# A block-sparse attention and gated MLP kernel: a planner's order replaced by a written list

## The chip, the cores and the metric

The kernel runs on one core of a Trainium2 chip. The core has a matrix engine (TensorE, here PE; its weight loads are shown as PEld), a vector engine (VectorE, DVE), an activation engine (ScalarE, ACT), a general engine (GpSimd, POOL) and a queue engine that only issues DMAs (SyncE, SP). Each engine takes its own instructions strictly in the order in which the program gives them; between engines, semaphores make one wait for another. Matrix results go to eight banks of PSUM, of 2 KB in each of 128 partitions. The metric is the device time of one execution in microseconds; lower is better.

## The reference

Four batches, eight heads, 768 positions of 64 numbers. Attention is block-sparse with blocks of 32 positions: a query block sees the block itself and its two neighbours, the first and the last block, and three blocks given at run time by `sampled_blocks`. The first and the last query block see everything. The attention output is then the input of a two-layer MLP over 3072 tokens.

```python
scores = scale * np.matmul(q, k.transpose(0, 1, 3, 2))
mask = np.abs(blk_i - blk_j) <= window          # window = 1
mask = mask | (blk_i == 0) | (blk_j == 0) | (blk_i == n_blocks - 1) | (blk_j == n_blocks - 1)
for qb in range(n_blocks):
    for kb in sampled_blocks[qb]:
        mask[qb * block:(qb + 1) * block, kb * block:(kb + 1) * block] = True
attn = softmax(np.where(mask, scores, -1e9))
x = np.matmul(attn, v)                          # then heads side by side: (3072, 512)
h = x @ w_in                                    # (3072, 2048)
g = h * (1.0 / (1.0 + np.exp(-beta * h)))
out = g @ w_out                                 # (3072, 512)
```

## The kernel before, in words

The work is cut into 1731 *tasks*. A task has a name, an engine (or two from which one is chosen), a guessed duration, the tasks that it depends on, the PSUM banks that it opens or closes, and a function that records its instructions, mostly one to a few dozen. The kinds, in the order in which data passes through them:

- `ldK`, `ldV`, `ldQ`: loads of half a batch's K, V or Q. For batch 0 they are issued on SP (768 KB each), for batches 1 to 3 on POOL. `castK`, `castQ`, `vperm`, `permV` on DVE turn them to 16 bits; `trK`, `trQ` transpose on PE (L632), `evK`, `evQ` evict (ACT or DVE). `vtab` writes V to a table in HBM, from which `vg` gathers the value blocks (SP; `vv` loads the block numbers into registers).
- `selb`, `selw`, `sel16`, `pick`, `pickv`: for the first four pairs the sampled value blocks are instead picked by a matmul with a selection matrix (L825). `mask`, `maskb`, `maskc` make the additive mask for doubled blocks.
- Attention works on 44 *pairs* of query blocks (11 per batch), all heads at once. For pair n: `kg` (POOL, L710) copies the sampled key blocks, `kn` (POOL or DVE) the fixed ones; `sc` is the score matmuls (mask L849, then L862; from pair 33 on some are done two pairs at a time); `mx` the row maxima (DVE, L884), `ex` the exponentials (ACT, L892); `hl` or `rc` the reciprocals (DVE); `nrm` the scaling (POOL or DVE, L915, from pair 11 on); `tp` eight transposes on PE (L929) and `ptv` their copy out (DVE or ACT); for pairs from 31 on one transposing DMA `tpd` on SP does both; `av` the product with the values (L971, from pair 16 on the wide form of L963; before pair 11 with the reciprocals' matmuls of L953); `rs`, `xv` put the result into the transposed activations `xT` (DVE or ACT). Buffers limit how far pairs can run ahead: three for keys and for probabilities, four or eight for values.
- The first and last block of a batch go through `gs`, `gm`, `ge`, `gr`, `gn`, `gt`, `gptv`, `gav`, `gx`, four units to a batch.
- The MLP takes the tokens in groups of 8, 8, 8, 16, 16, 16, 16 and 8 blocks of 32. For group G and each of 16 slices f, `hG.f` is four matmuls (L1155), `tanh` is on ACT (L1161), `stt` on DVE (L1166); then `yG.s.part`, four parts of four matmuls of 512 columns per 128 tokens (L1182), `oe` scales (ACT, L334) and `od` stores. `win` and `wout` are the weight loads, issued on POOL.

What sets the order: class `Plan` holds an event simulation. At each moment it gives each free engine the ready task with the lowest rank; the rank is a priority plus an offset from a table of tuned numbers. It chooses between two engines by which ends sooner by its guessed durations, and gives a task that opens banks the ones that are free longest. At most five banks go to the MLP while attention is left. The resulting order of tasks is then recorded, so that each engine has its instructions in that order. The plan's times have no effect beyond that order, the choice of engines and the banks.

Of the kernel before, what the change touches and what calls it, by code (L numbers as in the profile page):

```python
# [20 lines left out]
BIAS = {("nrm", "DVE"): 2.0, ("gn", "DVE"): 1.5}  # L21


class Task:
    def __init__(self, name, eng, dur, emit, deps=(), prio=0.0, lat=0.0,
                 opens=(), closes=(), moe=False, dma=0.0, slack=0.0, hw=0, bulk=None):
        self.on = {eng: dur} if isinstance(eng, str) else dict(eng)
        self.name, self.eng, self.dur, self.emit = name, None, None, emit
        self.deps = [d for d in deps if d is not None]
# [4 lines left out]
        self.tiling = Plan.TILING.get(self.kind, 0)  # L34
        self.end = None


class Plan:


    HOP = 0.18
# [3 lines left out]
    MARGIN, DMARGIN = 1.0, 1.0  # L45


    TILING = {"sc": 1, "gs": 1, "av": 2, "gav": 2, "trK": 2, "trQ": 2}
    CHANGE, KEEP = 0.1, 0.0
    YOUNG = {"PE": 0, "DVE": 0, "ACT": 0.0, "POOL": 0.5, "SP": 0.0}  # L50
    YIELD = 20

    OFFSET = {'gt': 5, 'gav': 10, 'trK': 7.6, 'oe': 2.2, 'vg': -0.6, 'vv': -14.0, 'pick': -1.2, 'av0': 0.8, 'ptv0': -3.8, 'xv0': 3.7, 'vg0': 0.9, 'sc1': -2.5, 'kg1': 12.5, 'kn1': -11.1, 'mx1': -15, 'vg1': -5, 'av2': -5, 'kg2': 2.8, 'kn2': 4.2, 'hl2': 5.2, 'rs2': -5, 'kg3': -11.2, 'ex3': 0.3, 'rs3': -0.6, 'kg4': -15, 'rs4': 7.8, 'kn5': 18.1, 'ptv5': 6.3, 'rs5': 39.6, 'av6': -0.3, 'kg6': 2.5, 'kn6': -60, 'ptv6': -2.4, 'mx6': 4.5, 'sc7': 15.7, 'tp7': 21.7, 'av7': 1.3, 'rs7': 1.6, 'sc8': 0.4, 'hl8': -3.7, 'xv8': -17.7, 'av9': -14.9, 'kg9': -6.0, 'kn9': 15, 'mx9': -15, 'ex9': -0.6, 'hl9': 19.8, 'rs9': 15, 'sc10': 21.3, 'tp10': 0.8, 'av10': 15, 'kg10': 2.9, 'kn10': -15, 'mx10': 30, 'vg10': 30, 'sc11': -60, 'av11': 15, 'ex11': 5, 'xv11': -1.7, 'av12': 0.5, 'kn12': -2.5, 'ptv12': 1.2, 'rs12': -0.3, 'xv12': 26.5, 'tp13': -0.2, 'kn13': 4.0, 'rs13': -3.7, 'xv13': -41.1, 'av14': 15, 'kg14': -15, 'kn14': -30, 'rs14': 24.8, 'xv14': 6.6, 'ptv15': 30, 'xv15': -24.7, 'mx0.0': 0.7, 'mx0.1': -9.9, 'mx1.1': -3.1, 'ex1.1': 5.7, 'ex2.0': -2.1, 'ex4.1': -15, 'mx7.1': 56.3, 'gn1': -22.5, 'vperm0.0': -0.6, 'trQ1': 11.7, 'trQ2': 11.1, 'trK3': 2.2, 'trQ3': -0.4, 'castQ': 2.6, 'tabK2': -34.6, 'tabK3': 8.6, 'ttQ2': 19.9, 'ldV3': 0.9, 'pick1': 9.2, 'pickv': 30, 'ldV0.1': 0.1, 'evK0': -6.3, 'evQ0': -1.2, 'tanh0': 5.1, 'stt1': -14.2, 'h3': 0.5, 'y3': -1.4, 'oe3': -8.0, 'y4': 1.4, 'tanh4': 9.0, 'oe4': 1.7, 'h5': 15.9, 'y5': -1.2, 'stt5': 3.2, 'h6': -60, 'y6': 11.9, 'tanh7': 60, 'stt7': -19.4}

    def __init__(self, n_banks, moe_banks):
        self.tasks = []
        self.n_banks, self.moe_banks = n_banks, moe_banks
        self.bank = {}
# [6 lines left out]
    def run(self):  # L65
        tasks = self.tasks
        attention_left = sum(1 for t in tasks if t.opens and not t.moe)
        succ = {}
        need = {}
        for t in tasks:  # L70
            need[t] = len(t.deps)
            for d in t.deps:
                succ.setdefault(d, []).append(t)
        readers = {}
        for t in tasks:
            for b in t.closes:
                readers[b] = readers.get(b, 0) + 1
        ready_at = {t: 0.0 for t in tasks}
        engines = sorted({e for t in tasks for e in t.on})
        free = {e: 0.0 for e in engines}  # L80
        waiting = {e: [] for e in engines}
        ring_at = hw_at = 1.0
        lanes = [0.0] * 8
        issued = 0

        tiling = 0
        off = {t: t.prio + self.OFFSET.get(t.name, self.OFFSET.get(t.name.split(".")[0], self.OFFSET.get(t.kind, 0.0)))
               for t in tasks}

        def rank(t, e):  # L90

            young = now - ready_at[t] < self.YOUNG[e] - 1e-9
            return off[t] + (self.KEEP if e == "PE" and t.tiling != tiling else 0.0) + (self.YIELD if young else 0.0)

        bank_free = [(0.0, i) for i in range(self.n_banks)]
        held_moe = 0
        moe_owner = set()
        events = []
        seq = 0

        def release(t):
            for e in t.on:
                waiting[e].append(t)

        for t in tasks:
            if need[t] == 0:
                release(t)
        now = 0.0
        order = []
        done = 0  # L110
        while done < len(tasks):
            progress = False
            for e in engines:
                if free[e] > now + 1e-9:
                    continue
                best = None
                for t in waiting[e]:
                    if ready_at[t] > now + 1e-9:
                        continue
                    if len(t.on) > 1:  # L120
                        cost = {o: max(free[o], now) + d + BIAS.get((t.kind, o), 0.0)
                                for o, d in t.on.items()}
                        if cost[e] > min(cost.values()) + 1e-9:
                            continue
                    if t.bulk is not None and ring_at > now + t.bulk + 1e-9:
                        continue
                    if t.opens:
                        n_ok = sum(1 for f, _ in bank_free if f <= now + 1e-9)
                        if n_ok < len(t.opens):
                            continue  # L130
                        if t.moe and attention_left and held_moe + len(t.opens) > self.moe_banks:
                            continue
                    if best is None or rank(t, e) < rank(best, e):
                        best = t
                if best is None:
                    continue
                t = best
                for other in t.on:
                    waiting[other].remove(t)
                t.eng, t.dur = e, t.on[e] * (1.0 if e == "PE" else self.MARGIN)  # L140
                if e == "PE" and t.tiling != tiling:
                    t.dur += self.CHANGE
                    tiling = t.tiling
                if t.opens:
                    bank_free.sort()
                    for name in t.opens:
                        _, i = bank_free.pop(0)
                        self.bank[name] = i
                        if t.moe:
                            held_moe += 1  # L150
                            moe_owner.add(name)
                    if not t.moe:
                        attention_left -= 1
                free[e] = now + t.dur
                end = now + t.dur + t.lat
                if t.hw:
                    at = now
                    for _ in range(t.hw):
                        at = max(at, lanes[issued % 8]) + t.dur / t.hw
                        begin = max(hw_at, at + 0.4)  # L160
                        both = max(0.0, ring_at - begin) / self.RING
                        work = self.DMARGIN * t.dma / t.hw
                        took = work / self.DIRECT if work <= both * self.DIRECT else work + both * (1 - self.DIRECT)
                        ring_at += (1 - self.RING) * min(took, both)
                        hw_at = begin + took
                        end = lanes[issued % 8] = hw_at + 0.9 + (self.LATER if ring_at > hw_at else 0.0)
                        issued += 1
                    free[e] = at
                elif t.dma:
                    begin = max(ring_at, end + 0.6)  # L170
                    both = max(0.0, hw_at - begin)
                    work = self.DMARGIN * t.dma
                    took = work / self.RING if work <= both * self.RING else work + both * (1 - self.RING)
                    ring_at = begin + took
                    end = ring_at + 1.1
# [1082 lines left out]
```

## Time and profile before

| | |
|---|---|
| runs shown | 300.73, 301.71, 305.26 us; median 301.71 |
| the profiled execution's span | 302.9 us (from the first to the last instruction) |
| busy PE | 279.5 us, 92%, 4109 matmuls |
| busy DVE, ACT, POOL | 237.5, 218.6, 170.0 us |
| mean granted clock of PE | 0.981 |
| DMA | 47.55 MB, mean 157 GB/s |

The profile is of one execution, of which the span is the time from the first to the last instruction; the durations used below are from it. Busy PE includes time in which a matmul's end is only modelled, so a busy PE need not be at its peak. A stretch's row gives each engine's busy time in it and the number of instructions, then the clock granted to PE as a share of full speed. A row of a group of instructions gives line, engine, operation, what is written from what, shapes and count, then the busy time and the mean of one in ns, then the idle time just before them and what ended it. A row in order of time gives the start and duration in us.

### The profile page before, as it was taken

The numbers are of one execution on the slowest core, as the hardware profiler recorded it, in microseconds if no ns is written. First come the engines' busy times: TensorE is split into PE (matmuls) and PEld (weight loads), VectorE is DVE, ScalarE is ACT, GpSimd is POOL, SyncE is SP. The second block draws the span as 40 slices with busy tenths as digits, with TensorE's granted clock in tenths as the row PEclk, the third lists the DMA queues.
The fourth block names the chain that finished last, engine by engine and source line by source line (L and its number), as shares of the span: only waits on it lengthen the run. The fifth ranks groups of instructions, "written<-read, shape, count | busy, mean of one in ns | idle before, by whom it ended". The sixth has DMA issues, their size and how long they took to land.

```text
span 302.9 us, 11451 instructions
## 1 busy us (share of the span) xinstructions
PE 279.5 (92%) x4109; PEld 173.8 (57%) x4109; DVE 237.5 (78%) x556; ACT 218.6 (72%) x641; POOL 170.0 (56%) x513
## 2 busy tenths in 40 slices
PE   2599879999998799999999999999999999999993
PEld 1465668758846576665556555545554544555671
DVE  5848987999899998999999739999888834762150
ACT  3357657888789598799889749896787768763360
POOL 5057995034579957899777538677976654000000
PEclk9999957999999999999999999999999999999999
DMA  7999999979978852299933643248465446541102
GB/s 248 365 294 171 205 232 231 228 142 265 213 126 167 181 192 72 84 173 162 237 99 106 202 154 106 67 110 167 120 158 119 126 106 181 137 121 53 53 36 69
DMA packets 57170, 47.55 MB, mean 157 GB/s; under 512 B 19733, under 2 KB 53142, under 8 KB 57114
## 3 DMA queue, kind: packets, MB, share of 16 engines
q1 hardware_dynamic: 44736, 35.48, 41.3%
q0 software_dynamic: 12320, 11.27, 24.7%
q8 instruction: 32, 0.52, 0.7%
q14 instruction: 24, 0.20, 0.2%
q10 hardware_dynamic: 58, 0.07, 0.1%
HBM read 45.23 MB, written 9.44 MB: 180 GB/s over the span
## 4 chain that ended last, share of the span: by engine, by line
PE 49%; DVE 23%; issue 7%; ACT 6%; POOL 6%; DMA 5%; POOLq 2%; SPq 0%; DVEq 0%; ACTq 0%
PE bank L1155 17%; PE bank L1182 14%; DVE ST L884 5%; PE bank L825 4%; DVE g L1166 4%; PE bank L929 3%; POOL KG L710 3%; DMA g<-in_k_dram 3%; DVE SG L1040 3%; POOL PP L915 2%; PE bank L963 2%; PE bank L971 2%; ACT PP L892 2%; PE bank L632 2%; ACT t L1161 2%
## 5 line engine op out<-in xcount | busy, mean ns | idle before, releaser
L1155 PE MATMUL bank<-xT,w_in_sb 128*128 128x256 f16 (+1 forms) x512 | 93.8, 330 | 1.5 <-DVE g L1166 1.5
L892 ACT ACTIVATE PP<-bank,ST 128x256 f16<-128x256 f32 x176 | 81.9, 482 | 15.1 <-DVE ST L884 10.1
L1182 PE MATMUL bank<-w_out_sb,g 128*128 128x512 f16 x384 | 92.0, 379 | 0.0
L1161 ACT ACTIVATE t<-bank,beta_sb 128x512 f16<-128x512 f32 (+1 forms) x128 | 71.0, 595 | 15.7 <-PE bank L1155 10.4
L915 POOL TENSOR_SCALAR PP<-PP,ST 128x256 f16<-128x256 f16 x132 | 63.4, 499 | 30.8 <-DVE ST L909 29.2
L1166 DVE SCALAR_TENSOR_TENSOR g<-t,bank 128x512 f16<-128x512 f16 (+1 forms) x128 | 67.0, 547 | 16.3 <-ACT t L1161 15.8
L1155 PEld LDWEIGHTS <-w_in_sb 128*128 128x128 f16 x512 | 54.4, 115 | 28.1 <-issue 4.1
L710 POOL COPY KG<-KT 128x64 f32 x264 | 52.4, 249 | 25.6 <-PE bank L862 10.5
L884 DVE TENSOR_REDUCE ST<-bank 128x2 f32<-128x512 f32 x88 | 57.6, 680 | 4.2 <-PE bank L862 3.8
L1182 PEld LDWEIGHTS <-g 128*128 128x128 f16 x384 | 35.0, 98 | 37.4 <-issue 3.5
L892 ACT ACTIVATION_READ_ACCUMULATOR PP<-bank,ST 128x1 f32 x176 | 37.4, 212 | 0.0
L1061 POOL TENSOR_SCALAR PG<-PG,SG 128x768 f16<-128x768 f16 x13 | 13.1, 1010 | 24.4 <-ACT PG L1049 15.2
L334 ACT ACTIVATE osb<-bank 128x512 f32<-128x512 f32 (+1 forms) x24 | 14.2, 590 | 16.1 <-PE bank L1182 16.0
L330 DVE COPY PT<-bank 128x1024 f16<-128x1024 f16 x30 | 20.4, 683 | 3.8 <-PE bank L929 3.6
L330 DVE CAST xT<-bank 64x256 f16<-64x256 f32 (+1 forms) x35 | 14.6, 418 | 9.9 <-PE bank L963 6.8
L929 PE MATMUL bank<-identity,PP 128*128 128x128 f16 x248 | 20.4, 225 | 1.2 <-ACT KT L328 0.6
L963 PEld LDWEIGHTS <-VG 128*128 128x128 f16 x448 | 16.1, 98 | 9.2 <-issue 4.3
L1049 ACT ACTIVATE PG<-bank,SG 128x384 f16<-128x384 f32 x32 | 18.3, 589 | 4.2 <-DVE SG L1042 3.6
L929 PEld LDWEIGHTS <-PP 128*128 128x128 f16 x248 | 16.2, 101 | 6.0 <-issue 1.1
L963 PE MATMUL bank<-PT,VG 128*128 128x64 f16 x448 | 17.5, 193 | 2.2 <-DMA PT<-PP 1.5
L330 POOL COPY KG<-KT 128x384 f32<-128x384 f32 (+3 forms) x43 | 16.6, 411 | 1.3 <-PE bank L862 1.3
L328 ACT CAST xT<-bank 64x256 f16<-64x256 f32 (+1 forms) x30 | 11.3, 375 | 8.2 <-PE bank L1089 3.9
(119 smaller groups left out, 317.9 us busy)
## 6 DMA issues: line engine op xcount, KB each, us to landing
VG<-VT SPq DMA_DIRECT2D x220, 32.0 KB, 2.6
VG<-VT SPq DMA_DIRECT2D x32, 192.0 KB, 2.7
out_dram<-osb SPq DMA_DIRECT2D x20, 256.0 KB, 2.1
RV<-in_v_dram POOLq DMA_DIRECT2D x6, 384.0 KB, 6.6
RK<-in_k_dram POOLq DMA_DIRECT2D x6, 384.0 KB, 6.2
VT<-Vn SPq DMA_DIRECT2D x3, 768.0 KB, 3.4
RQ<-in_q_dram POOLq DMA_DIRECT2D x6, 384.0 KB, 6.3
w_in_sb<-in_moe_w_in_dram POOLq DMA_DIRECT2D x8, 256.0 KB, 8.8
```

What stands on the lines that cost most here:

```text
L330: (nc.vector if eng == "DVE" else nc.gpsimd).tensor_copy(out=out, in_=in_)
L710: nc.gpsimd.tensor_copy(out=kg32[:, g, :, (SR + r) * W:(SR + r + 1) * W], in_=kt32[:, :, bass.ds(vals[3 * g + r], W)])
L884: mx[n, u] = add(f"mx{n}.{u}", "DVE", 0.6, lambda n=n, u=u, sb_=sb_: nc.vector.tensor_reduce(out=sb_[:, 0, 2 * u:2 * u + 2], in_=bank(("S" ...
L892: nc.scalar.activation(out=pb[:, u, g, :], in_=bank(("S", n, u))[:, g * 256:(g + 1) * 256], func=AF.Exp, bias=sb_[:, 0, 2 * u + g:2 * u + ...
L915: (nc.vector if eng == "DVE" else nc.gpsimd).tensor_scalar(out=pb[:, u, g, :], in0=pb[:, u, g, :], scalar1=sb_[:, 2, 2 * u + g:2 * u + g + ...
L929: nc.tensor.transpose(out=o[:, s * P:(s + 1) * P], in_=pb[:, u, g, c * P:(c + 1) * P], identity=identity)
L963: nc.tensor.matmul(o[:, (g * NHP + hp) * 2 * BLK:(g * NHP + hp + 1) * 2 * BLK], lhsT=vgb[:, g, c, hp * P:(hp + 1) * P], rhs=pt[:, g, c, :, ...
L1049: nc.scalar.activation(out=pg[:, :].rearrange("x (j p) -> x j p", j=J)[:, :, hf * hw_:(hf + 1) * hw_], in_=bank(("GS", m, hf))[:, 0:S // 2 ...
L1155: nc.tensor.matmul(o[:, 0:TW], lhsT=w_in_v[:, c, f // 4, f % 4, :], rhs=xT[:, c, c0:c0 + TW], start=(c == 0), stop=(c == NHP - 1))
L1161: lambda G=G, f=f, TW=TW, tt=tt: nc.scalar.activation(out=tt[:, 0:TW], in_=bank(("H", G, f))[:, 0:TW], func=AF.Tanh, bias=0.0, scale=beta_ ...
L1166: lambda G=G, f=f, TW=TW, tt=tt, gg=gg: nc.vector.scalar_tensor_tensor(out=gg[:, f, 0:TW], in0=tt[:, 0:TW], scalar=1.0, in1=bank(("H", G, ...
L1182: nc.tensor.matmul(o[:, :], lhsT=gg[:, f, s * P:(s + 1) * P], rhs=w_out_sb[:, f, :], start=(f == 0), stop=(f == N_FFC - 1))
```

## The change

The event simulation goes. A string, ORDER, lists all 1731 tasks by name, each with the engine (A, D, G for ACT, DVE, POOL) where there is a choice, and with the PSUM banks that it opens. `Plan.run` reads the list, sets engine and banks, and returns the tasks in that order. The guessed durations in the task definitions change too, but nothing reads them any more; a new task kind for loading key block numbers ahead is defined and switched off (`NKL = 0`). So the instructions are the same apart from the form that an engine needs, and what differs is the order on each engine, the engine of 93 tasks, and the banks.

```diff
+ORDER = """
+selc sbl ldK0.1 ldK0.0 ldV0.1 ldV0.0 ldQ0.0 idx srow ident iota selb0:0 castK0.2 castK0.3 selb1:1 selw0 mask.0
+trK0.3:2 selw1 evK0.3:A sel16.2 castK0.0 sel16.0 trK0.0:2 castK0.1 evK0.0:A sel16.4 trK0.1:1 vperm0.1 trK0.2:0
...
+tpd33 gm15 y3.2.3 xv31.1:D kg37 ge15 vg34.0 nrm34:D h4.12:7 vg35.3 vg35.4 oe3.3 av32:5 gm14 h4.10:2 vres34:G xv32.0:A
...
+stt7.15 stt7.13 y7.0.2 stt7.14 y7.0.3 y7.1.1 oe7.0 y7.1.2 od7.0 y7.1.3 rows:6 oe7.1 of7.1 rowlist od7.1ACT od7.1SP
+"""
...
-    OFFSET = {'gt': 5, 'gav': 10, 'trK': 7.6, ...
...
     def run(self):
-        tasks = self.tasks
-        attention_left = sum(1 for t in tasks if t.opens and not t.moe)
...
+        by = {t.name: t for t in self.tasks}
+        full = dict(A="ACT", D="DVE", P="PE", G="POOL", S="SP")
         order = []
...
+        for word in ORDER.split():
+            name, _, place = word.partition(":")
+            t = by[name]
+            t.eng = full[place[0]] if place and place[0] in full else next(iter(t.on))
+            t.dur = t.on[t.eng]
+            for b, i in zip(t.opens, place.lstrip("ADPGS")):
+                self.bank[b] = int(i)
+            order.append(t)
         return order
...
-    plan = Plan(8, 5)
+    plan = Plan()
```

How the list stands against the old order, in the parts that the prediction speaks of:

- Start: the loads of batch 0 are in the order K, K, V, V, Q, then (behind the V table's two stores) Q; before it was V, V, K, K, Q, then Q behind the stores. The dummy activation `table` moves from the start to the middle; the ACT table load itself stays ahead of ACT's first copy.
- PE up to `sc0`: four `trK`, `pick1.0`, `trQ0.0`, `pick1.1`, `maskb`, `pick0.0`, three `trQ`, `pick2.1`, then `sc0`. `rows` moves from the start of PE's queue to its very end, `betaT` behind `av2`.
- PE's order between attention and MLP: up to `av12` the old order had 36 `h` and 16 `y` tasks, the new one 18 `h` and no `y`. In the old order `h0.0` came after `av4`, in the new one after `sc10`. The last MLP groups are interleaved differently, with `y` of groups 5 and 6 among `h` of 6 and 7.
- POOL: the weight loads (`win`, `wout`) are spread between the `kg` of pairs 3 to 17, with loads of batch 1 among them; before, all sixteen stood ahead of `kg11`.
- Engines of tasks: `ptv` 12 from DVE to ACT and one back; `xv` 15 from DVE to ACT, 11 back; `evK`, `evQ` 7 to ACT, 4 to DVE; `pickv` 2 to ACT, one back; `rs` 2 to ACT, 3 back; `nrm` 7 from POOL to DVE; `kn` 12 from DVE to POOL, 7 back; `vres` 3 from DVE to POOL; `gn` three each way.
- Eight banks as before, dealt from the list.

More of the change, by code (lines that the diff above doesn't have):

```diff
@@ L43 @@
     DIRECT, RING, LATER = 0.25, 0.7, 2.5
-    MARGIN, DMARGIN = 1.0, 1.0
     TILING = {"sc": 1, "gs": 1, "av": 2, "gav": 2, "trK": 2, "trQ": 2}
[L49 to L53, printed above, removed]
@@ L80, in run @@
[L80 to L93, printed above, removed]
```

362 lines of the change are left out of this document (173 added, 189 removed).

## The prediction

> **What bounds the kernel now.** I read the granted clock first, then busy time by stretch, then the chain of waits, then the instructions of the first 42 us in order of time. The stretches, busy time of each engine (instructions in brackets), granted clock, DMA share and GB/s:
>
> ```profile
> core 0: us, PE busy (x) PEld busy (x) DVE busy (x) ACT busy (x) POOL busy (x), PEclk, DMA share, GB/s
> 0.00:10.00 10.00, 1.94 (x9) 1.06 (x9) 5.43 (x22) 2.44 (x4) 3.85 (x24) 1.00 0.80 279
> ...
> 30.00:40.00 10.00, 7.04 (x261) 5.18 (x259) 9.39 (x22) 7.27 (x29) 9.87 (x36) 0.93 1.18 211
> 40.00:50.00 10.00, 10.00 (x177) 8.23 (x163) 7.46 (x22) 6.01 (x24) 8.76 (x25) 0.55 1.11 233
> 50.00:60.00 10.00, 10.00 (x181) 7.91 (x180) 9.60 (x28) 8.23 (x26) 0.00 (x0) 1.00 1.19 226
> ...
> 100.00:110.00 10.00, 7.20 (x149) 5.49 (x148) 10.00 (x19) 7.26 (x24) 7.08 (x23) 1.00 0.74 198
> ...
> sum 303.00, PE 279.53 PEld 173.75 DVE 237.46 ACT 218.61 POOL 170.02; mean PE 9.32 PEld 5.79 DVE 7.92 ACT 7.29 POOL 5.67
> ```
>
> The reader is to see that PE is the bound nearly everywhere: 279.5 of 303 us busy. What another order can win lies where PE idles or is slow: 8.1 us in the first stretch, 3.0 at 30 to 40, 2.8 at 100 to 110, and the stretch of 40 to 50 at clock 0.55 (some 4 us of work lost there although PE counts as busy). DVE stands above 9 of 10 from 50 to 170. At the end nothing but PE matters; the chain of waits (start, duration, what) shows its pace there:
>
> ```profile
> 255.21 13.97 PE bank L1155 x64
> 269.18 0.93 PE bank L963 x32
> ...
> 287.02 4.37 PE bank L1155 x40
> 291.38 6.92 PE bank L1182 x32
> ```
>
> A 512-column matmul costs 13.97/64 = 0.218 (L1155) or 6.92/32 = 0.216 us (L1182), a 256-column one 4.37/40 = 0.109, an av of the wide kind 0.93/2 = 0.47. From 298.3, the chain's end, to 302.9 come the last scaling and the output DMA: 4.6 us.
>
> **The change, part by part.** Instructions are the same, so the sum is made of *when PE can start what*. All that PE is given is in-order; work on PE that waits is lost for good, because the work itself is conserved.
>
> *The head.* The new list loads K first, then V, then Q; the old one V, K, Q. DVE in order of time (start, duration, line, tiles, what ended the idle time) gives the landings:
>
> ```profile
> 5.49 0.96 DVE L330 CAST Vn<-xT 128x1536 f16<-128x1536 f32 x1 [0.94 <-DMA xT<-in_v_dram]
> 7.61 0.96 DVE L330 CAST Vn<-xT 128x1536 f16<-128x1536 f32 x1 [0.17 <-DMA xT<-in_v_dram]
> 9.70 1.03 DVE L538 CAST RK<-g 128x768 f16<-128x768 f32 x2 [0.80 <-DMA g<-in_k_dram]
> 13.88 1.03 DVE L538 CAST RQ<-g 128x768 f16<-128x768 f32 x2 [0.30 <-DMA g<-in_q_dram]
> 18.37 1.07 DVE L538 CAST RQ<-g 128x768 f16<-128x768 f32 x2 [0.21 <-DMA g<-in_q_dram]
> 24.13 1.29 DVE L884 TENSOR_REDUCE ST<-bank 128x2 f32<-128x512 f32 x2 [1.05 <-PE bank L862]
> ```
>
> A half of 768 KB lands every 2.1 us, so K lands at 5.5 and 7.6, V at 9.7 and 11.8, the first half of Q at 13.9 as before. The second half of Q is issued behind both stores of the V table on SP, as before, and I leave it at 18.4. Keys are ready some 3 us earlier. But V's last cast ends at 12.8 and two selections of about 0.35 follow, so pick1.0, PE's first large work, starts at 13.5 against 14.0. The four picks, eight transposes and maskb before sc0 then give: pick1.0 at half speed to 16.2, trQ0.0 16.9, pick1.1 18.9, pick0.0 20.3, three trQ at 0.36, pick2.1 1.36, hence sc0 at about 22.9 instead of 23.4. The first max follows 0.7 later, the first exponential another 0.7 later: **ACT starts its softmax work at 24.3.** The table warm-up that moved late costs nothing: the table load itself still stands ahead of the first copy, at the launch.
>
> *The middle, where the new list differs most.* Before pair 12's output (av12) the old list had put 36 H matmul groups and 16 Y groups; the new one puts 18 H groups and no Y, and all of attention's steps up to pair 12 instead. So PE will not be the bound there; the engines that feed attention are. The reassignments make ACT the fullest: 12 transposed copies (ptv) go from DVE to ACT and one back, ACT gets a net 3 K evictions and 4 more xv copies. Over the kernel that is about +13.6 us for ACT and -10.9 for DVE. ACT by shape, and two exponentials in order of time:
>
> ```profile
> L1161 ACT ACTIVATE t<-bank,beta_sb 128x256 f16<-128x256 f32 x64 | 28.6, 488 | 10.4 <-PE bank L1155 5.8 <-DVE g L1166 3.8 <-PE bank L862 0.2
> L1049 ACT ACTIVATE PG<-bank,SG 128x384 f16<-128x384 f32 x32 | 18.3, 589 | 4.2 <-DVE SG L1042 3.6 <-DVE SG L1057 0.3
> L328 ACT COPY KT<-bank 128x768 f16<-128x768 f16 x12 | 9.6, 817 | 6.4 <-PE bank L632 6.4
> L334 ACT ACTIVATE RS<-bank 128x256 f32<-128x256 f32 x9 | 3.5, 384 | 5.0 <-PE bank L971 4.8
> L328 ACT COPY PT<-bank 128x1024 f16<-128x1024 f16 x1 | 1.0, 1020 | 0.0
> ```
>
> ```profile
> 24.85 0.47 ACT L892 ACTIVATE PP<-bank,ST 128x256 f16<-128x256 f32 x1 [0.23 <-DVE ST L884]
> ...
> 26.66 0.49 ACT L892 ACTIVATE PP<-bank,ST 128x256 f16<-128x256 f32 x1
> ```
>
> Two ex tasks lie between these two starts: 1.81/2 = 0.905 each. Neighbours on ACT overlap by about 0.1, so I take 0.1 off each mean; a ge scales from ex to 1.12. From ex0.0 to ptv12 the new list gives ACT 30 ex (27.2), 16 tanh of 256 columns at 0.39 (6.2), 6 ge (6.7), 7 ptv at 0.91 (6.4), 8 K and Q evictions at 0.71 (5.7), 8 rs at 0.28 (2.2), 4 pickv, half a ptv's columns, at about 0.5 (1.9), one gx (0.3): **56.6 us**. With no idle at all ptv12 ends at 24.3 + 56.6 = 80.9, and av12 starts 0.2 later. Can ACT be that dense? Added up in the same way, DVE is done with the max for ex14.0 some 3 us before ACT wants it, and GpSimd with the keys of that pair 6 us before. The idle is bounded by nothing and, at the old density of about 8.3 of 10 in 50 to 60 (when ACT was not the bound), by 11.6 us. I take 1.9, near the lower end, since no input is late by the sums. **av12 starts at 83.0.**
>
> *What is left for PE.* From av12 on: 96 Y groups, 384 matmuls at 0.216 = 83.0; 64 H groups of 512 columns at 0.218 x 4 = 55.9; 46 H groups of 256 columns, 184 at 0.109 = 20.1. For the small steps, PE in order of time:
>
> ```profile
> 115.09 0.68 PE L971 MATMUL bank<-PT,VG 128*64 128x32 f16 x32
> 115.70 0.28 PE L849 MATMUL bank<-maskr,ones 64*32 64x192 f16 x8
> 115.79 0.40 PE L862 MATMUL bank<-KG,QT 64*32 64x256 f16 x16
> 116.13 0.63 PE L1155 MATMUL bank<-xT,w_in_sb 128*128 128x256 f16 x4
> ```
>
> From start to start a score step takes 0.43 (115.70 to 116.13); a tp I put at 0.45, by its 8 matmuls against the score step's 24. So 23 score steps, five of them double, 11.3; 18 tp 8.1; 32 av 15.3 (28 at 0.47, four at about 0.52); the rest of attention, 32 small steps of 0.3 to 0.9, 13.3. Together 207.0 us. A change of the array's tiling costs about 0.1 (the av at 115.09 took 0.61 to the next start), half of it already in the steps; the new list has 51 changes from here on: 2.6. Other PE waits from here: the stretch of 100 to 110 alone cost 2.8 in the old run; later ones were small. I take 3.0, between 0 and 8.
>
> *Costed at nothing, with their cover.* Weights come later on GpSimd's queue: win0.0 is issued near 46 instead of 25, and a quarter took 8.8 us to land, so h0.0 may wait from 49.5 to 54; ACT wants its first tanh only at 56.7. Without that cover, each further us of landing is a us lost. The vg gathers on SP keep their number; SP is in order too, so one that waits for an old pair's av holds those behind it. Pair n from 12 on waits for the av of pair n-4, which the new list, too, puts well ahead; without that distance the av behind is late by as much as the gather. The seven nrm that go to DVE have no row there; four 128x256 scalings lie between 0.4 (a quarter of the GpSimd time of 4 x 0.5) and 2.0 each, I take 0.9. The last steps (rows, rowlist) stand behind the output's scaling and delay nothing by more than 0.3.
>
> **Sum:** 83.0 + 207.0 + 2.6 + 3.0 + 4.6 = 300.2 us of span, against 302.9. The median of the runs shown is 301.71, 1.2 below the profiled span, so I forecast 299.0 us, 0.9% less.
>
> **The rivals.**
>
> *Dense queues (faster).* If ACT idles 0 and PE waits 0 behind av12, the sum falls by 4.9 to 295.3 of span, 294.1 us. For it: GpSimd stood still from 50 to 60 in the old run while DVE was full, and the new list has work on every engine there. Against it: three in-order queues feeding each other have never all been above 9 of 10 in any stretch shown.
>
> *PE too sparse, half clock (slower).* Stretches of 3.41 us around the slow part of the old run:
>
> ```profile
> 35.26:38.67 3.41, 1.38 (x32) 0.79 (x31) 3.31 (x9) 3.36 (x16) 3.29 (x15) 1.00 1.16 238
> 38.67:42.08 3.41, 2.54 (x55) 1.94 (x57) 3.34 (x8) 2.60 (x12) 3.38 (x16) 0.50 1.20 239
> 42.08:45.50 3.42, 3.42 (x75) 3.03 (x72) 2.54 (x8) 1.01 (x5) 2.79 (x11) 0.50 1.09 224
> ...
> 103.53:106.94 3.41, 1.94 (x33) 1.50 (x32) 3.41 (x5) 1.00 (x4) 3.41 (x11) 1.00 0.33 104
> ```
>
> PE busy for 1.38 of 3.41 us was followed by about 10 us at 0.50; 1.94 of 3.41 was not. In the new list PE has, by the sums, 24.6 us of work between sc1 and sc12, from 25 to 63: 0.65 of the time, with holes (waiting for av2 near 40, for av4 near 52) that come under 1.4 in a stretch. If all 38 us ran at half clock, PE would need 49: 11 us late, 311.2 of span, 310.0 us. It decides from about three slow spells of 10 us; one or two are absorbed, since ACT is the bound there.
>
> [...]
>
> *PE's code arrives late (no change or slower).* In the old run sc7 began, stopped and went on:
>
> ```profile
> 37.11 0.25 PE L849 MATMUL bank<-maskr,ones 64*32 64x192 f16 x1
> 39.54 0.36 PE L849 MATMUL bank<-maskr,ones 64*32 64x192 f16 x7 [2.17 <-DVE ST L884]
> ```
>
> A step cut in the middle, with DVE's part long done, looks like instructions missing: by then PE had run about 960, counting weight loads. The new list needs 1458 before h0.0 at 49.5; the old one 1202 before h0.0 at 45. If supply is the limit, some 3 us more: 302.0 us.
>
> **How the numbers follow.** Forecast 0.51, dense queues 0.27, half clock 0.17, late code 0.05. No change means within 2% (295.7 to 307.7), about what a measurement of this kernel can tell. Dense queues give faster 0.27; half clock gives slower, with 0.01 of late code: 0.18; the rest 0.55. The range goes from the dense case less 1.6 for a head that starts earlier than I have it, to 308, where ACT's idle reaches two thirds of its upper bound: 292.5 to 308.
>
> **What would show it.** Score step of pair 0 at 22 to 24 us; ACT above 9 of 10 from 25 to 80 and GpSimd no longer empty at 50 to 60; pair 12's av at 81 to 86; from there PE idle under 4 us until the end; tail again 4.6. Wrong if ACT idles more than 6 us before av12, if the clock row shows three or more tenths near 5, or if PE idles again between 90 and 150, where GpSimd, DVE and PE are all nearly full in the new list.

## The result and the profile after

The four executions of the new list took 311.38, 314.01, 316.58 and 317.37 us, median 315.29, against a median of 301.22 before (four executions, 300.32 to 305.26). The ratio is 1.036, with a 95% interval of 1.030 to 1.042; it leaves out executions more than 1.5% above the fastest of their kernel. The forecast was 299.0 us, and the range ended at 308: wrong, and on the wrong side. The profiled execution is the fastest, 311.38 us with a span of 309.5, so what the profile shows is 6.6 of span against the profile of before, the smaller part of the difference. One reason is that the profile of before is of a long execution: time is 1.8 to 1.9 us more than span in the new list, and by that a span of 302.9 stands for about 304.8 us. The rest of the difference lies in executions of the new list that left no profile, only a span and a mean granted clock.

The stretches of both profiles, in the columns of the prediction, first of before, then of after:

```profile
0.00:20.00 20.00, 10.85 (x98) 7.18 (x99) 13.25 (x46) 7.54 (x11) 8.23 (x42) 1.00 0.94 311
20.00:60.00 40.00, 37.04 (x744) 27.24 (x744) 33.15 (x86) 28.84 (x99) 24.07 (x77) 0.87 1.12 215
60.00:80.00 20.00, 20.00 (x373) 14.80 (x368) 19.32 (x56) 16.61 (x45) 10.36 (x22) 1.00 0.98 203
80.00:110.00 30.00, 26.37 (x508) 17.67 (x506) 28.52 (x62) 23.88 (x79) 21.46 (x62) 1.00 0.85 181
110.00:290.00 180.00, 176.97 (x2371) 102.63 (x2366) 140.54 (x303) 138.87 (x403) 105.91 (x311) 1.00 0.51 126
```

```profile
0.00:20.00 20.00, 11.88 (x87) 6.34 (x89) 11.02 (x34) 6.63 (x9) 10.77 (x41) 1.00 0.95 309
20.00:60.00 40.00, 31.06 (x664) 20.98 (x666) 32.88 (x87) 34.05 (x112) 26.78 (x97) 0.90 1.11 217
60.00:80.00 20.00, 14.46 (x413) 12.10 (x411) 13.12 (x33) 13.87 (x43) 11.19 (x35) 0.87 0.72 126
80.00:110.00 30.00, 27.44 (x570) 20.30 (x565) 27.30 (x73) 26.71 (x88) 22.61 (x59) 1.00 0.89 172
110.00:290.00 180.00, 179.59 (x2313) 109.32 (x2312) 138.75 (x311) 141.02 (x398) 96.93 (x277) 1.00 0.54 132
```

Take from each stretch the time in which PE was not busy, and add what the clock took (length times one minus the clock). Before: 9.2, 3.0, 0, 3.6, 3.0 us, and 5.2 by the clock. After: 8.1, 8.9, 5.5, 2.6, 0.4, and 6.6. The new list loses 11.5 us more between 20 and 80 us and 1.4 more by the clock; it wins 4.7 elsewhere. That makes 8.2 us, where the span grew by 6.6; the ledger is good to about 2 us (changes of tiling, 106 in the new list against 142, are not in it), and it says where to look: 20 to 80 us. The trace has no clock event ahead of 18.2 us before and 17.6 after, so the clock of 1.00 in the first row of each is not measured there. The profiled execution also has the highest clock of the four: span times one minus the mean clock is 7.7 us for it (0.975) and 10.3 us for the one of 314.01 (0.967), where the old order's executions in the rounds below average 3.6 to 4.6.

The chain of waits of the kernel after has the largest hole in a few lines (start, duration, what):

```profile
57.91 1.16 PE bank L1132 x6
59.07 0.29 issue
59.36 4.60 DMA w_in_sb<-in_moe_w_in_dram
63.96 0.05 issue
64.00 0.53 PE bank L1132 x3
64.54 0.29 issue
64.83 4.31 DMA w_in_sb<-in_moe_w_in_dram
69.18 0.40 PE bank L1132
```

```profile
59.36 0.71 POOL L527 DMA_DIRECT2D w_in_sb<-in_moe_w_in_dram  x1 [0.62 <-PE bank L1132]
64.83 0.76 POOL L527 DMA_DIRECT2D w_in_sb<-in_moe_w_in_dram  x1 [2.15 <-PE bank L1132]
```

```profile
64.00 0.52 PE L1132 MATMUL bank<-xT,w_in_sb 128*128 128x256 f16 x3 [1.03 <-DMA w_in_sb<-in_moe_w_in_dram]
69.18 0.40 PE L1132 MATMUL bank<-xT,w_in_sb 128*128 128x256 f16 x1 [3.75 <-DMA w_in_sb<-in_moe_w_in_dram]
```

L1132 is the H matmul (L1155 before), L527 the load of `win`. The second fence is GpSimd in order of time, the third PE: the load `win1.0` waited for a matmul of `h0.1`, then `h0.2` waited for that load; `win1.1` waited for `h0.2`, then `h0.3` for it. PE, DMA and GpSimd take turns: PE stood 1.03 and 3.75 us for the two loads, GpSimd 0.62 and 2.15 us for the two matmuls, and what is queued behind on either stood too. None of h0.0 to h0.3 reads what `win1` brings. `win1.0` writes columns 512 to 1023 of two row blocks in one DMA; the stretch of memory from its first to its last byte encloses columns 0 to 511 of the second block, which every h0 matmul reads there. The list puts `win1.0` behind h0.1 and `win1.1` behind h0.2, so the program has a wait in each direction. Before, all of `win` stood ahead of h0.0.

### The profile page after: what moved, and what is told of

Read it like the earlier page. It is cut to its first block, busy times and chain, and to the rows that moved or that the text cites. A ratio compares the mean times of both kernels' runs of the same rounds, so it can differ in the third digit from the quotient of the medians.

```text
span 309.5 us, 11393 instructions
## 1 busy us (share of the span) xinstructions
PE 279.6 (90%) x4109; PEld 177.6 (57%) x4109; DVE 227.2 (73%) x546; ACT 228.8 (74%) x659; POOL 168.3 (54%) x505
## 4 chain that ended last, share of the span: by engine, by line
PE 72%; DMA 9%; DVE 8%; ACT 6%; issue 2%; SPq 1%; ACTq 0%; DVEq 0%
PE bank L1159 26%; PE bank L1132 24%; PE bank L939 4%; PE bank L905 4%; PE bank L602 4%; DMA xT<-in_v_dram 3%; DMA w_in_sb<-in_moe_w_in_dram 3%; ACT PP L868 3%; PE bank L837 2%; PE bank L947 2%; DMA VG<-VT 2%; PE bank L824 2%; DVE ST L860 2%; PE bank L1046 2%; DVE SG L1017 2%
## 5 line engine op out<-in xcount | busy, mean ns | idle before, releaser
L1132 PE MATMUL bank<-xT,w_in_sb 128*128 128x256 f16 (+1 forms) x512 | 96.8, 328 | 8.0 <-DMA w_in_sb<-in_moe_w_in_dram 4.8
L868 ACT ACTIVATE PP<-bank,ST 128x256 f16<-128x256 f32 x176 | 81.7, 485 | 10.3 <-DVE ST L860 6.3
L891 POOL TENSOR_SCALAR PP<-PP,ST 128x256 f16<-128x256 f16 x104 | 49.7, 494 | 50.9 <-DVE ST L885 18.9
L1132 PEld LDWEIGHTS <-w_in_sb 128*128 128x128 f16 x512 | 54.4, 114 | 36.8 <-issue 5.9
L1159 PEld LDWEIGHTS <-g 128*128 128x128 f16 x384 | 35.7, 98 | 38.9 <-issue 2.9
L868 ACT ACTIVATION_READ_ACCUMULATOR PP<-bank,ST 128x1 f32 x176 | 38.2, 217 | 0.0
L300 POOL COPY KG<-KT 128x384 f32<-128x384 f32 (+3 forms) x60 | 23.1, 414 | 18.9 <-ACT KT L298 11.5
L905 PE MATMUL bank<-identity,PP 128*128 128x128 f16 x248 | 19.6, 226 | 0.1
L824 PE MATMUL bank<-maskr,ones 64*32 64x192 f16 (+1 forms) x352 | 12.8, 260 | 7.0 <-ACT VG L298 3.2
L300 DVE CAST xT<-bank 64x256 f16<-64x256 f32 (+1 forms) x31 | 12.8, 417 | 7.9 <-PE bank L939 4.9
L837 PE MATMUL bank<-KG,QT 64*32 64x256 f16 x704 | 16.7, 269 | 0.4 <-DVE KG L300 0.4
L1017 DVE TENSOR_REDUCE SG<-bank 128x1 f32<-128x384 f32 x32 | 16.2, 546 | 0.4 <-PE bank L1003 0.3
```

Source lines behind the costliest of these rows:

```text
L300: (nc.vector if eng == "DVE" else nc.gpsimd).tensor_copy(out=out, in_=in_)
L837: nc.tensor.matmul(bk[u][hp * BLK:(hp + 1) * BLK, g * 256:(g + 1) * 256], lhsT=QT[b % 2][u * D:(u + 1) * D, hp, (i0 + g) * BLK:(i0 + g + 1 ...
L868: nc.scalar.activation(out=pb[:, u, g, :], in_=bank(("S", n, u))[:, g * 256:(g + 1) * 256], func=AF.Exp, bias=sb_[:, 0, 2 * u + g:2 * u + ...
L891: (nc.vector if eng == "DVE" else nc.gpsimd).tensor_scalar(out=pb[:, u, g, :], in0=pb[:, u, g, :], scalar1=sb_[:, 2, 2 * u + g:2 * u + g + ...
L905: nc.tensor.transpose(out=o[:, s * P:(s + 1) * P], in_=pb[:, u, g, c * P:(c + 1) * P], identity=identity)
L1132: nc.tensor.matmul(o[:, 0:TW], lhsT=w_in_v[:, c, f // 4, f % 4, :], rhs=xT[:, c, c0:c0 + TW], start=(c == 0), stop=(c == NHP - 1))
```

## The experiments

All are the written list with tasks moved, unless said otherwise; the old order was written as such a list too, with the old engines and banks. "Old" and "new" are these two lists. Each ratio is to the kernel before, run again in the same round; its median lay between 301.2 and 303.5 us.

### The two weight loads put late into the old order

```diff
 (old)  h0.0 rs4 mx6.1 h0.1
+win1.0
 ...  h0.2
+win1.1
```

> The old order with only these two loads moved behind h0.1 and h0.2, as the new list has them. Weight theory: h0.2 and h0.3 wait for the landing of each, 4 to 5 us apiece, in a place where PE has work queued behind them: 5 to 10 us slower than before, 306 to 311 us. Rival (PE's sparseness in the new list is the cause, the loads are covered until h0.4): within 2 us of before.

Measured: 314.18 us against 303.02, ratio 1.039 (1.032 to 1.046). More than expected, and as much as the whole change costs. PE's waits and the matmuls in order of time:

```profile
PE bank L1136 <- DMA w_in_sb<-in_moe_w_in_dram: 10.2, 2, 5.2
```

```profile
52.48 1.47 PE L1136 MATMUL bank<-xT,w_in_sb 128*128 128x256 f16 x6 [5.17 <-DMA w_in_sb<-in_moe_w_in_dram]
58.95 0.41 PE L1136 MATMUL bank<-xT,w_in_sb 128*128 128x256 f16 x1 [5.00 <-DMA w_in_sb<-in_moe_w_in_dram]
```

Two tasks in another place of one queue are worth 11 us where PE has work behind them.

### The same, with the loads cut so that they enclose nothing

```diff
-nc.gpsimd.dma_start(out=w_in_sb[:, c:c + 2, fs], in_=w_in_r[:, c:c + 2, fs])
+for e in (c, c + 1):     # win1.0 and win1.1 only
+    nc.gpsimd.dma_start(out=w_in_sb[:, e:e + 1, fs], in_=w_in_r[:, e:e + 1, fs])
```

> The old order with win1.0 and win1.1 behind h0.1 and h0.2, as in the run that took 314 us, but each cut into two DMAs of one 128-row block, as in the new list with cut loads. If the enclosing stretch is what makes loads and matmuls wait for each other, h0.2 and h0.3 wait for nothing and the loads are issued when GpSimd gets there; only h0.4, the first real reader at 50 us, may wait 2 to 4 us for the landing: 303 to 308. If the late place alone costs it, 312 to 316.

Measured: 312.45 us against 302.81, ratio 1.036 (1.028 to 1.043). The mechanism is as said, the time not: h0.2 and h0.3 wait for nothing, and the waits move to h0.4, the first reader.

```profile
49.49 0.30 PE L1139 MATMUL bank<-xT,w_in_sb 128*128 128x256 f16 x1 [1.26 <-DMA w_in_sb<-in_moe_w_in_dram]
54.24 0.40 PE L1139 MATMUL bank<-xT,w_in_sb 128*128 128x256 f16 x1 [3.57 <-DMA w_in_sb<-in_moe_w_in_dram]
```

The total wait on weights falls from 10.2 to 6.3 us, the time by only about 2. Overlap makes the wait in the one place, true lateness in the other; of the 11 us, some 2 are the overlap's.

### The loads mended in the new list

```diff
 (new, early loads)  kn10 [+win1.0 +win1.1] ... h0.1 [-win1.0] ... h0.2 [-win1.1]
 (new, cut loads)    order unchanged, the cut of above
 (new, early loads and vg0)   vg0.1 vg0.2 vg0.0 moved from ahead of pick0.0 behind pickv0.0
 (new, loads still earlier)   ldV1.0 win0.0 rowc win1.0 kg10 win1.1 ldQ1.0 kg8 win2.0 ldQ1.1 kn10, and vg0 as above
```

> The new list with two entries moved: the weight loads win1.0 and win1.1 go from behind h0.1 and h0.2 to behind kn10, where GpSimd stood idle from 48.6 to 52.8 us. Weight theory: PE's waits of 1.0 us in h0.2 and 3.75 us in h0.3 go, ACT's 1.3 and 3.5 us of idle go with them, and av12 comes 5 to 7 us earlier (87 to 89 instead of 93.6); time 5 to 9 us under the new list's 315, so 306 to 310 us. Rival, sparse PE and half clock: the wait is only one hole among many, at most 2 us less, 313 to 316.

> The new list unchanged, but win1.0 and win1.1 are each two DMAs of one 128-row block instead of one DMA of two, so that the stretch of memory from the first to the last byte that one DMA writes no longer holds columns that h0.1 to h0.3 read; place and bytes are the same. If the wait came only from that overlap of enclosing stretches, the loads wait for no matmul and the matmuls for no load, and the time is that of the run with the early loads within 2 us (306 to 311). If h0.2 and h0.3 needed the data, or the load's lateness by itself was the cause, it stays at 313 to 317.

> The run with the early loads, and besides the gather of values vg0 (three DMAs on SP) moved behind pickv0.0, so that pickv1.1 on ACT no longer waits for it (ACT stood 2.6 us before 24.6, PE 2.2 us before sc2). ACT's first exponential comes at 23.9 to 24.5 instead of 25.55, av12 1 to 1.5 us earlier than in the run with early loads: 1 to 2 us less time. If ACT is not the bound of this stretch, no difference.

> The new list with win0.0, win1.0 and win1.1 loaded right behind ldV1.0 (some 41 to 45 us, ahead of Q of batch 1) and vg0 behind pickv0.0. Theory that each of the two waits is a loss of its own: no PE wait for weights, 304 to 308. Rival, that PE has so little to do here that a mended wait is followed by the next one (code, gathers, banks) and by half clock: 309 to 314, as with the three mended lists before.

Measured, as ratios to before: 1.017 (1.009 to 1.026; 311.05 us), 1.035 (1.026 to 1.043; 313.54), 1.036 (1.029 to 1.042; 313.54) and 1.030 (1.021 to 1.039; 310.40). The new list itself had 1.036. So the loads mended in four ways give back between nothing and 2% of a loss of 3.6%; the 2% is the least sure, as the five executions of that run lie between 307.07 and 313.68 us. The theory that this wait was the loss by itself falls in its size. With the cut loads no matmul waits for a weight between 20 and 100 us, and other waits stand there instead:

```profile
PE bank L953 <- DMA VG<-VT: 2.8, 1, 2.8
PE bank L953 <- issue: 2.5, 1, 2.5
```

With vg0 moved as well, ACT's first exponential came at 24.37 as expected, but the time rose by 2.5 us over that of the early loads instead of falling by 1 to 2. In the last of the four, PE's idle time from 60 to 80 falls from 5.5 to 1.3 us as it should, and av12 comes at 88.6 instead of 93.6; but from there to the end it takes 219.8 us instead of 215.9. Behind 110 us PE's idle time rises from 0.4 to 3.4, for one thing by waits for gathered values:

```profile
PE bank L942 <- DMA VG<-VT: 2.6, 2, 2.0
```

### Is ACT the bound, as the forecast's sum had it?

Twenty ACTIVATEs of pairs 3 to 12 left out, in both orders (in the new one on top of the early loads).

```diff
-for g in range(2):
+for g in range(1 if 3 <= n <= 12 else 2):
     nc.scalar.activation(...)
```

> The run with the early loads, and for pairs 3 to 12 only the exponentials of the first query block of each pair are computed (20 of 40 ACTIVATEs left out; the second block's probabilities are stale). That takes 20 x 0.45 = 9 us from ACT ahead of av12 and gives no engine anything. Theory that ACT is what the front of the new list runs against: av12 4 to 8 us earlier and 4 to 8 us less time than the 311 us of the run with early loads, 303 to 307. Rival, that the front waits on other things (code, gathers, DVE's maxima): at most 2 us less, 309 to 311.

> The same 20 exponentials left out of the old order. There PE is the bound up to 90 us by its trace: 0 to 2 us less than before, 300 to 302. If ACT set the time there too, 4 us less or more.

Measured: new 313.59 us, ratio 1.036 (1.030 to 1.042); old 303.23 against 303.51, ratio 0.998 (0.994 to 1.002). ACT's busy time in the stretch that the forecast gave to it, in the new list and in the lightened one:

```profile
24.30:94.00 69.70, 60.22 (x194) 0.90 0.98 185
```

```profile
24.30:94.00 69.70, 54.84 (x160) 0.88 1.02 192
```

5.4 us less work on ACT in that stretch (6.3 less than in the profile of the early loads), and no gain in time: the ratio is that of the new list, and above the 1.017 of the early loads. av12 began at 91.1 us, against 92.9 with the early loads and 93.6 in the new list, so 1.8 to 2.5 us earlier and not 4 to 8. ACT was full because it was waited through, not because it was the bound. This is the step on which my number rested.

### Is it PE's code?

> The run with the early loads, and the additive masks of pairs 0 to 14 left out (120 matmuls and their weight loads, 240 instructions of PE, about one packet of code; the result lacks those masks). Theory that PE's code comes too late (the waits of 1.8, 1.6 and 1.9 us with no releaser in that run): they go or halve, 4 to 6 us less than the 311 us of the run with early loads: 305 to 307. Rival, ACT is the bound and PE only follows: 0 to 1.5 us less, 309 to 312.

```diff
 def emit_sm(n=n, p=p):
+    if n < 15:
+        return
```

Measured: 310.36 us, ratio 1.025 (1.016 to 1.035), against 1.017 for the run with early loads: no gain, though PE has 240 instructions less to run. PE's waits with no releaser do fall as the theory has it, from 6.5 to 2.1 us between 20 and 120 us, and the time doesn't follow; so at this size code supply doesn't set the time. It seems to make single waits, in the new list too:

```profile
PE bank L1132 <- issue: 2.0, 1, 2.0
```

This wait runs from 95.1 to 97.1 us, and a packet of 16 KB on the instruction queue begins at 94.8. That the one is the cause of the other is inferred from the times.

### Order or engines?

Each of the 93 reassigned tasks put back in the new order, and put forward in the old.

```diff
 (new, old engines)  -ptv0:A +ptv0:D ... -nrm13:D +nrm13:G ...   (93 tasks)
 (old, new engines)  -ptv0:D +ptv0:A ... -nrm13:G +nrm13:D ...
```

> The new list's order and places, with each of the 93 reassigned tasks back on its old engine. Theory that a full ACT makes each late input cost: seven ptv (6.7 us) and some evictions leave ACT ahead of av12, which comes 3 to 6 us earlier; 309 to 312. Rival, the order alone sets it (weights' wait, DVE as full as ACT): 313 to 317.

> The old order with the new engines for the 93 tasks. Theory that the order is what costs: PE stays the bound, within 3 us of before, 300 to 306. Rival, the new engines are what costs: 308 or more.

Measured: the new order with old engines 321.71 us, ratio 1.063 (1.058 to 1.068); the old order with new engines 317.02, ratio 1.049 (1.044 to 1.054). The first is above both of its branches; the second is in the branch of the rival (308 or more), which the first contradicts. Each order is worse with the other's engines, by 6 and by 15 us. Order and engines can't be priced apart; the two changes to the whole don't add.

### Front of the one, back of the other

The old list up to av16, av27 or av35, then all that is left in the new order, with banks dealt to fit.

```diff
 (old)  ... av16
-      what follows in the old list
+      what is left of the new list, in its order
```

> The old order up to av16, and from there all remaining tasks in the new list's order (banks dealt so that none is opened before it is closed). In the trace of before PE loses some 9.8 us behind 110 us against its own fastest paces, in that of the new list 2.7. Theory that the new list is bad ahead of av12 and good behind av16: 5 to 7 us less than before, 295 to 298. Rival, that its back is tight only because the front left 27 more MLP groups to fill it: 300 to 306, no better than before.

> The old order up to av27 (178 us), the rest in the new order. Behind 180 us PE loses 5.3 us in the old trace and 1.5 in the new. The front has done 16 Y groups (14 us) more than the new list at that place, which the back then lacks. If the other engines have room there (ACT 6 to 9, DVE 5 to 9.6 of 10), 2 to 4 us less than before: 298 to 300; if the lack decides, as it did in the joint at av16, 304 to 310.

> The old order up to av35 (225 us), the rest in the new order; the MLP work done by then differs by 2 us. Behind 225 us PE loses some 2.8 us in the old trace and 0.6 in the new: 1 to 3 us less than before, 299 to 301. If the new back end depends on the new front, 302 or more.

Measured: 314.99 (ratio 1.039, 1.032 to 1.046), 315.47 (1.043, 1.036 to 1.050) and 306.66 us (1.012, 1.006 to 1.018). None gains, and the first two are slower than either branch had it. The stretch behind the joint at av16, first in the profile of before, then with the new back:

```profile
110.00:160.00 50.00, 49.89 (x864) 31.30 (x859) 48.25 (x109) 44.06 (x139) 41.71 (x122) 1.00 0.64 135
```

```profile
110.00:160.00 50.00, 41.09 (x728) 25.83 (x727) 43.21 (x104) 40.58 (x141) 40.30 (x125) 0.86 0.52 112
```

The new back end is dense (0.4 us of PE idle from 110 to 290) because its front leaves MLP groups undone: 27 at av16, 17 at 0.44 us and 10 at 0.86, 16 us of PE work. With the old front, which has done them, the same order leaves PE 9 us idle in 50 and slows its clock. So the 2.6 us won behind 110 us seem to have been paid for ahead of it. What the joint itself costs isn't known: at av35, where little MLP work differs, the new back still lost 1.2%.

### What the half clock costs, and what brings it

```diff
 (old)  rows, rowlist to the very end; betaT, betah behind tp4; ahead of tp3:
+for _ in range(8):
+    nc.tensor.matmul(free_bank[:, :], lhsT=identity, rhs=Vn[0][:, 0, :], start=True, stop=True)
```

> The old order with 8 extra matmuls of 512 columns (into a free bank, their result unused) ahead of tp3, where PE stood waiting between 36 and 39.5 us; rows and betaT move behind them, so that the number of PE instructions ahead of that place is the same. Theory that a stretch of 3.4 us with PE busy under about 0.6 is what brings the half clock, and that the spell costs: the stretch comes to 0.8, the spell of 38.7 to 48.9 us (4.7 us of PE work) does not come, 2 to 4.5 us less than before, 298 to 301. Rival, that the clock falls anyway or that other engines set this part: 301 to 304.

Measured: 302.74 us against 301.93, ratio 1.003 (0.999 to 1.007). Three stretches of that profile:

```profile
35.30:38.70 3.40, 3.18 (x63) 1.67 (x55) 3.28 (x8) 2.85 (x13) 3.40 (x15) 1.00 1.18 250
38.70:49.00 10.30, 8.51 (x192) 7.30 (x176) 8.93 (x26) 7.14 (x27) 9.28 (x29) 1.00 1.13 233
95.00:106.00 11.00, 7.89 (x158) 6.22 (x156) 10.90 (x22) 7.30 (x24) 9.70 (x29) 0.96 0.89 224
```

At this place the first half of the theory holds: with PE busy for 3.18 of 3.40 us, the clock stays at 1.00 where it had gone to 0.50. The second isn't borne out: the spell, priced at 4.7 us of PE work, is gone from the profile, and the time is the same. In the two profiles the H matmuls start some 2.2 us earlier than before up to 104 us, and 1.0 us earlier at 112. So half of the price was won, and half of that was given back around 105, where DVE is busy 10.90 of 11 us and a short spell falls (0.96 in the third row). The test is also smaller than it looks: by their mean granted clocks, the executions lost 2.5 us to the clock on average, those of the old order in the same round 3.6, so about 1 us of loss was taken away and not 4.7. Over 51 executions of the old order, each microsecond lost to the clock went with some 0.5 us of time (correlation 0.58 within rounds). What a spell costs stays open.

### The MLP's pace exchanged

The attention order of the one list with the MLP's tasks at the pace of the other, banks dealt anew; and, as a control of that dealing, the old list with nothing but the banks dealt anew.

```diff
 (new attention)  av4
+h0.0 h0.1 tanh0.0 ...        the MLP tasks that the other list has there
```

> The new list's attention order and engines, with the MLP's tasks put at the old order's pace (as many per finished pair) and the weight loads as early as there; banks dealt anew. Theory that holding back the MLP is what makes PE idle and its clock fall between 20 and 100 us: idle there falls from 17.0 us to under 9, time 301 to 306. Rival, the attention order or its engines: 311 to 317.

> The reverse: the old attention order, engines and weight loads, with the MLP's tasks at the new list's pace; banks dealt anew. Theory that holding back the MLP costs: PE idles 10 us or more between 20 and 100, time 308 to 316. Rival: 300 to 305.

> The old order and engines, unchanged, only with the PSUM banks dealt by the rule that the two runs with exchanged MLP pace used (the free bank that was closed earliest in the list). If that rule is harmless, 300 to 305, and their 390 us came from the interleaving; if it is what jammed them, 320 or more.

Measured: 390.06, 390.54 and 302.86 us (ratio of the last 1.001, 0.998 to 1.005). The first two lie far outside every branch of their expectations. The banks are harmless; the interleaving is not. My rule put every tanh and every scaling close behind its matmul on ACT's and DVE's queues as well, and the in-order queues jammed. In the second of the two, DVE stood 84.5 us on ACT's tanh alone. That says nothing about the pace, so whether holding back the MLP costs by itself stays open.

```profile
DVE g L1146 <- ACT t L1141: 84.5, 56, 9.1
```

### The profiles side by side

PE not busy in four stretches, and what the clock took up to 290 us, worked out as above (us). The two jammed lists are left out, and the early loads, whose profile is of their longest execution, 2.6 us above the median:

| list | median | 20-60 | 60-80 | 80-110 | 110-290 | clock |
|---|---|---|---|---|---|---|
| before (profile shown first) | 301.2 | 3.0 | 0.0 | 3.6 | 3.0 | 5.2 |
| old, PE kept busy | 302.7 | 2.8 | 0.0 | 3.4 | 2.6 | 1.8 |
| old, banks anew | 302.9 | 5.2 | 0.0 | 3.3 | 3.6 | 1.6 |
| old, 20 exponentials less | 303.2 | 3.4 | 0.0 | 3.5 | 3.9 | 5.2 |
| old, new engines | 317.0 | 3.9 | 1.4 | 1.8 | 10.1 | 7.0 |
| old, late loads | 314.2 | 12.6 | 0.0 | 0.5 | 3.7 | 10.2 |
| old, late loads, cut | 312.5 | 8.6 | 0.0 | 1.6 | 4.8 | 6.8 |
| old to av16, then new | 315.0 | 3.1 | 0.0 | 1.7 | 9.3 | 12.4 |
| old to av27, then new | 315.5 | 2.9 | 0.0 | 1.4 | 10.6 | 10.6 |
| old to av35, then new | 306.7 | 4.1 | 0.0 | 1.4 | 6.0 | 3.4 |
| new | 315.3 | 8.9 | 5.5 | 2.6 | 0.4 | 6.6 |
| new, cut loads | 313.5 | 9.5 | 4.3 | 3.1 | 0.7 | 9.9 |
| new, loads and vg0 | 313.5 | 8.8 | 3.8 | 1.5 | 3.5 | 10.0 |
| new, loads still earlier | 310.4 | 9.6 | 1.3 | 2.5 | 3.4 | 5.2 |
| new, 20 exponentials less | 313.6 | 9.6 | 3.1 | 3.6 | 1.6 | 10.4 |
| new, masks less | 310.4 | 10.7 | 1.4 | 2.6 | 1.4 | 7.0 |
| new, old engines | 321.7 | 13.2 | 6.7 | 3.8 | 3.3 | 8.6 |

One column sorts the fronts. From 20 to 60 us PE idles 2.8 to 5.2 us in every list that starts with the old order and has its weights early, and 8.8 to 13.2 in every list that starts with the new one, whatever is mended. The 6 us there belong to the new front: to its attention order or to the MLP work that it holds back, and not to its engines alone (13.2 with the old ones). Split at 45 us, where the old list starts its H matmuls (the new one at 57.9), first before, then after:

```profile
20.00:45.00 25.00, 22.04 (x501) 15.38 (x500) 20.35 (x49) 16.79 (x60) 19.65 (x69) 0.87 1.10 206
45.00:60.00 15.00, 15.00 (x246) 11.86 (x246) 12.80 (x38) 12.05 (x39) 4.42 (x9) 0.87 1.15 229
```

```profile
20.00:45.00 25.00, 18.59 (x418) 11.16 (x419) 20.15 (x51) 20.90 (x72) 18.84 (x69) 1.00 1.13 215
45.00:60.00 15.00, 12.47 (x246) 9.82 (x247) 12.73 (x37) 13.16 (x41) 7.94 (x28) 0.73 1.09 220
```

Up to 45 us PE's idle time and the clock together take 6.2 us before and 6.4 after; from 45 to 60 they take 2.0 and 6.6. So the gap opens where the old list has H matmuls for PE and the new one has none. That fits the held-back MLP as a cause, and no run here tests it. Which wait of the new front matters isn't settled either: PE's largest ones from 20 to 60 us are for banks that ACT frees late, and lightening ACT didn't shorten them (6.4 us in the new list, 6.6 in the lightened one).

```profile
PE bank L824 <- ACT VG L298: 3.2, 3, 2.2
PE bank L824 <- ACT PG L1026: 2.2, 3, 1.6
PE bank L824 <- ACT PP L868: 1.0, 2, 0.6
```

## Why the prediction was wrong, point by point

- **The head.** Right: sc0 began at 22.45, forecast 22 to 24. But ACT's first exponential came at 25.55, not 24.3. Two copies of picked values stood ahead of it and waited for a gather, and not for its data: with the gather moved behind them (early loads and vg0) they ran at 22.37. That this is again an enclosing stretch is likely, and not tested:

```profile
24.59 1.07 ACT L298 CAST VG<-bank 96x512 f16<-96x512 f32 x2 [2.61 <-DMA VG<-VT]
```

- **The middle, the step that failed.** The sum made ACT the bound from its first exponential to ptv12, with 56.6 us of work and 1.9 of idle, and put av12 at 83.0. It began at 93.6. From the two copies to the end of ptv12 (24.6 to 92.5 us) ACT's work was about right, 58.8 us; its idle time was 9.2. The row that I had, 8.3 of 10, was near (8.6 of 10 came), and my own upper bound of 11.6 held; I chose the lower end because added-up queues had no late input, which they show only if no queue ever stands. Of the 10.6 us, 7.3 are this idle time and 2.2 the work. With ACT lightened and nothing gained, the sum also had the wrong bound. What the runs show in its place is waits of PE, ACT, DVE and DMA for each other in turn, of which the lockstep on the two loads is the largest on the chain behind the head (8.9 us); mending it gave back at most about half, and what sets the rest stays open.
- **"Costed at nothing": the weights.** I priced their lateness at h0.0 (49.5 to 54, covered until ACT's first tanh). h0.0 indeed waited for no load; h0.2 and h0.3 did. The step looked at when data land, and not at what the moved load is ordered against. The rows of the kernel after name both waits, h0.2's for the load and the load's for a matmul of h0.1.
- **What is left for PE.** Right: from av12 to the end 217.2 us were forecast, 215.9 came (309.5 less 93.6), in the profiled execution, the fastest. PE's idle time from av12 on was 2.4 us, against the 3.0 that I took: 2.0 up to 110 us and 0.4 behind it.
- **The rivals.** *Half clock* has the nearest number (310.0), by accident: its spells came (0.90 and 0.87 in the rows), but took 1.4 us more than before in the profiles and some 3 to 7 by the mean clocks, not 11. Whether they cost time or only mark PE's idleness isn't settled. *Late code* falls at the size tested. *Dense queues* falls. The rival that was missing is a transfer put into lockstep with the work that it was meant to run beside; by the mended lists it is worth at most some 2 of the 3.6%.
- **The range.** Its upper end came from ACT's idle alone. Spreading 16 loads along an in-order queue deserved a bound of its own from a row that I had: 8.8 us to land, for each load that something might stand behind.

## What to carry to other kernels

When a list moves a transfer behind a reader of the same tensor, read the waits of both in the built program before pricing it: a strided transfer can be ordered against columns that it doesn't touch, and the two waits then close a loop through the DMA (4.6 and 4.3 us on the chain here). A load moved late can also simply be late: the two together cost the old list 11 us, and cutting the loads gave back 2. Don't call the fullest engine the bound; take work from it and see. And a gain ahead of the next full engine can be given back there (here around 105 us, where DVE was busy 10.90 of 11), as a dense end may have been paid for by a sparse start (0.4 us of PE idle behind 110 us in the new list, 9.3 with the old order up to av16).

## What the runs showed of the hardware

The clock fell after stretches in which PE was far from idle. Of the kernel after, in stretches of 3.41 us:

```profile
41.47:44.88 3.41, 2.04 (x56) 1.20 (x56) 3.24 (x11) 3.40 (x13) 3.35 (x14) 1.00 1.22 261
44.88:48.29 3.41, 3.27 (x62) 3.05 (x62) 3.13 (x12) 3.41 (x15) 3.12 (x12) 0.50 1.26 210
55.12:58.53 3.41, 1.42 (x51) 0.88 (x30) 3.27 (x11) 2.81 (x8) 1.43 (x8) 1.00 0.98 294
58.53:61.95 3.42, 3.42 (x56) 2.68 (x57) 2.99 (x11) 3.16 (x13) 2.76 (x8) 0.50 0.81 170
```

PE busy for 2.04 of 3.41 us (0.60) was followed by a fall, and so was 1.42 (0.42). With PE kept busy in the old order, 1.77 of 3.50 us (0.51, from 101.70) was followed by one; before, 1.94 of 3.41 (0.57, from 103.53) was not. So a fall did not go by this share alone. From 58.53 the clock was back after one stretch at 0.50, with PE busy for 3.42 of 3.42; before, it was not back after the wholly busy stretch at 42.08, but after the next one. What sets the clock is not shown by these rows.
